# Batch 0's loads first: a gate on the summed k, w_in's second half in two DMAs, and a new order for group 0's second product

## The chip, the cores and the metric

The kernel runs on one core of a Trainium2 chip. The metric is the device time of one execution in microseconds. The kernel before has a median of 301.65 us over 5 runs (301.26 to 301.77). One further execution was profiled; it took 302.63 us, of which the profile's span is 300.8 us.

## The reference

Pooled attention over 8 batches and 8 heads feeds a two-layer network. Keys and values are averaged over blocks of 8 rows, so 576 queries meet only 72 keys:

```python
# q, k, v: (8, 8, 576, 64); w_in: (512, 2048); w_out: (2048, 512); all float32
k_p = k.reshape(B, H, 72, 8, D).mean(axis=3)
v_p = v.reshape(B, H, 72, 8, D).mean(axis=3)
attn = softmax(q @ k_p.T / 8)            # over the 72 keys
x = (attn @ v_p).transpose(0, 2, 1, 3).reshape(4608, 512)
out = gelu_tanh(x @ w_in) @ w_out        # (4608, 512) float32
```

## The kernel before, in words

**Tiling.** The attention's result is held transposed and in bf16 as `xT` (128 rows, 4 row blocks `ko`, 4608 columns). The network works on 9 groups of 512 columns, `g` = 0 to 8. In each group the *first product* (`p1_mm`, line 402) makes 16 blocks `fo` of the hidden layer, each from 4 matmuls over `ko`; ScalarE applies the gelu (`gelu`, line 408) into `gT`. The *second product* (`p2_mm`, line 411) makes 4 row tiles `r` of the output, each from 16 matmuls over `fo`; VectorE copies the sum to SBUF and SP stores it (`store`, lines 417 to 425). A matmul of 512 columns takes 0.216 us when they follow each other.

**Where attention lies.** Batch 0's attention is done alone, before the first group. Batch `g + 1` is done beside group `g`: its sums of k and v and its transposes beside the first product (the table `side`, by `fo`), its scores, exponentials, weighted sums (`av`, `av_main`) and multiplications (`mult`) between the matmuls of the second product (the table `todo`, by the place `m` in `seq`). All orders are written out by hand; every engine works through its own instructions in program order.

**Loads.** GpSimd issues q, w_in, w_out and later batches' k and v on one queue (q0 in the profile); loads that change float32 to bf16 (q, w_in, w_out) are all there. Batch 0's k and v and their remainders are issued by SP and ACT (q1 and q10). At the start GpSimd issues without any wait: q of batch 0 in two parts, w_in in two halves of two `ko` rows each (line 118), k, the remainders and q of batch 1, and w_out in four quarters of four `fo` each (line 125). There are eight semaphores for GpSimd's DMAs, and a ninth DMA waits until the one eight before it has landed; so line 125's four issues wait for both parts of q and both halves of w_in. Batch 1's v is issued by SP (line 496) after some fills on VectorE. `load_next` then loads batch 2: its q, a transposing DMA of it on SP (line 261), a small copy on GpSimd called `gate` that waits for that transpose (line 516), and behind it k and v (lines 82 to 93). Batch 2's k is summed on VectorE (line 154), transposed by a DMA on SP (line 182, into `kx`), and read by `rem_scores` (line 301) at `m` = 2 of group 1's second product.

**Batch 0's order.** k is summed (`k_steps`), transposed on TensorE and copied by VectorE (lines 217, 224, 232); the scores follow, their exponentials on ScalarE, the sums of exponentials (`den0`) and their inverses by a logarithm and an exponential (lines 359, 361). Then v is summed (`v_steps`, line 154, into `vz`), the weighted sums `av0` (line 368) and the multiplications `mult0` (line 372) fill `xT`, and group 0's first product begins. `spin` (line 431) are filler matmuls.

**Group 0.** The first 12 matmuls of its first product use `ko` 0 and 1 for `fo` 0 to 5; then come `ko` 2 and 3, block by block. Its second product goes over all four row tiles with `fo` 0 to 7 and then over all four with `fo` 8 to 15. Since only two banks of PSUM are free for it, row tiles 0 and 1 are cut: their first half is copied to SBUF (`sums`, line 639) and added when the second is stored (line 420).

Of the kernel before, what the change touches and what calls it, by code (L numbers as in the profile page):

```python
# [18 lines left out]
def kernel(  # L19
# [49 lines left out]
    def load_k(b, engs):  # L69
        rows = k[b].rearrange("h (j l) d -> (h j) (l d)", l=8)  # L70
        main = rows[0:128 * KR].rearrange("(p r) c -> p r c", r=KR)
        n = KR // len(engs)
        for i, eng in enumerate(engs):
            eng.dma_start(out=kts[b % 2][:, i * n:(i + 1) * n], in_=main[:, i * n:(i + 1) * n])
        engs[0].dma_start(out=kts[b % 2][64:128, KR], in_=rows[128 * KR:])
        rows = v[b].rearrange("h (j l) d -> j h (l d)", l=8)
        engs[-1].dma_start(out=kts[b % 2][0:64, KR], in_=rows[64:])  # L77
# [36 lines left out]
    load_q(0, 1, 2)  # L114
    make_identity(nc, identb)

    def load_w_in(i):
        nc.gpsimd.dma_start(out=w_in_b[i], in_=w_in_v[:, 2 * i:2 * i + 2])

    load_w_in(0)  # L120
    load_w_in(1)
    load_k(1, [nc.gpsimd])
    load_q(1)
    for i in range(4):
        nc.gpsimd.dma_start(out=w_out_b[:, 4 * i:4 * i + 4, :].rearrange("p j d -> p (j d)"), in_=w_out_v[:, i])
    gate = consts.tile([1, 2], BF16, name="gate")


    xT = consts.tile([128, KO, N], BF16, name="xT")
# [125 lines left out]
    def trans_q(b, i, t0, n, bank, eng):  # L255
        trans_q_mm(b, i, t0, n, bank)
        trans_q_copy(b, i, t0, n, bank, eng)
# [4 lines left out]
                                    in_=qs[b].rearrange("p i c -> p (i c)"))  # L262

    QG = [(0, 0, 5), (0, 5, 4), (1, 0, 5), (1, 5, 4)]


    es = {}
# [170 lines left out]
    def scores(c, pr, bank):  # L438
        qk(0, c, pr, bank)
        expo(0, c, pr, bank)  # L440
# [3 lines left out]
    trans_q(0, *QG[0], 5, nc.scalar)  # L444
    trans_q(0, *QG[1], 6, nc.vector)
    trans_k_copy(0, 1, 4, upper=False)
    scores(0, 0, 2)
    scores(0, 1, 0)
    spin(2, 7)
# [40 lines left out]
        nc.vector.memset(t[:, KR + 1], 0.0)  # L490
    nc.vector.memset(kTs[1][0], 0.0)
    nc.vector.memset(kTs[1][1], 0.0)

    for i in range(2):
        nc.vector.memset(vts[1][:, 2 * i, 0:1], 0.0)
    load_v(1, [nc.sync], 2)
    for w in vps:
        nc.vector.memset(w, 8.0)
    nc.gpsimd.memset(kz, 0.0)

    for fo, ko in [(fo, ko) for fo in range(6) for ko in range(2)]:
# [3 lines left out]
    for g in range(NG):  # L505
        nb = g + 1 if g + 1 < B else None
        act_set(GELU_SET)

        def load_next():

            if nb >= KX:
                nc.gpsimd.tensor_copy(out=gate, in_=eT[64:65, H - 1, 1, 0:2])  # L512
            if nb < KX:
                load_q(g + 2)
                trans_q_dma(g + 2)
                nc.gpsimd.tensor_copy(out=gate, in_=qTs[g + 2][0:1, 1, TP - 1, 0:2])
            if g + 2 >= KX:
                load_k_dma(g + 2)
            else:
                load_k(g + 2, [nc.gpsimd])  # L520
            load_v(g + 2, [nc.gpsimd])
            if nb >= KX:
                load_q(g + 2)

        if 0 < g and nb is not None and nb < KX:
            load_next()


        side = {fo: [] for fo in range(FO)}
        if nb is not None:  # L530
            kk = k_steps(nb) if nb < KX else k_steps_dma(nb)
            tk = [lambda: trans_k(nb, 4)]
            if nb > KX:
                kk.append(lambda: trans_q_dma(nb))
            kk.append(lambda: v_moves(nb))
            vv = v_steps(nb)
            if nb >= KX:
                plan = {0: kk, 7: vv[:1], 8: vv[1:]}
            elif g:
                plan = {2: kk[:1], 3: kk[1:], 7: vv[:1], 8: vv[1:], 9: tk}  # L540
            else:
                tq = [lambda a=a, i=i: trans_q(nb, *a, (5, 6, 7, 5)[i], nc.vector) for i, a in enumerate(QG)]
                plan = {0: kk[:-1], 11: kk[-1:], 12: tk, 13: tq[:1], 14: tq[1:2], 15: tq[2:3]}
            for fo, what in plan.items():
                side[fo] += what

        if g + 1 == NG:

            gLs = [kts[i // 2].rearrange("p r c -> p (r c)").bitcast(BF16)[:, i % 2 * 512:i % 2 * 512 + 512]
                   .rearrange("p (f c) -> p f c", f=4) for i in range(4)]  # L550
            for i, o in enumerate(gLs):
                side[4 * i + 3].append(lambda i=i, o=o: nc.vector.tensor_copy(  # L552
                    out=o.rearrange("p f (x t) -> p f t x", t=4),
                    in_=gTs[g][:, 4 * i:4 * i + 4, 384:].rearrange("p f (t x) -> p f t x", t=4)))

        if g == 0:
            first = [(fo, ko) for fo in range(6) for ko in (2, 3)]
        else:  # L560
            late = 3
            rest = [fo for fo in range(4) if fo != late]
            kos = (0, 2, 1) if g == 1 else (0, 1, 2)
            first = [(fo, ko) for ko in kos for fo in rest]
            first += [(fo, ko) for fo in (late, 4) for ko in kos]
            first += [(fo, 3) for fo in rest + [late, 4]]
        for fo, ko in first:
            p1_mm(g, fo, ko)
        for fo in range(FO):
            if fo >= (5 if g else 6):  # L570
                for ko in range(KO):
                    p1_mm(g, fo, ko)
            gelu(g, fo)
            for s in side[fo]:
                s()

        if g == 0:
            load_next()


        todo, sums = {}, {}

        def at(m, f, *a):
            todo.setdefault(m, []).append((f, a))

        if nb is not None:
            act_set(EXP_SET)
        if nb is not None and nb >= KX:
            at(2, rem_scores, nb)
            at(2, rem_expo, nb)  # L590

            pairs = [(0, 0), (0, 1), (1, 0), (1, 1), (0, 2), (1, 2), (0, 3), (1, 3)]
            for pr, m in enumerate((6, 17, 31, 45)):
                at(m, main_scores, nb, pr)
            for n, m in enumerate((13, 22, 28, 34, 40, 51, 56, 62)):
                at(m, av_main, nb, *pairs[n], 4 + 2 * (n % 2))
            scalar = [(6, 0, 0), (6, 1, 0), (13, 0), (18, 0, 1), (18, 1, 1), (22, 1), (28, 2), (33, 0, 2), (33, 1, 2),
                      (34, 3), (40, 4), (46, 0, 3), (51, 5), (51, 1, 3), (56, 6), (62, 7)]
            for m, *x in scalar:
                if len(x) == 2:  # L600
                    at(m, main_expo, nb, *x)
                else:
                    at(m, norm, nb, *pairs[x[0]], 4 + 2 * (x[0] % 2))
            for n, m in enumerate((24, 30, 36, 44, 49, 57, 64, 65)):
                at(m, mult, nb, *pairs[n], 4 + 2 * (n % 2))
            if g + 2 < B:
                at(3, load_next)
        elif nb is not None:
            if g == 0:
                at(2, trans_q, nb, *QG[3], 5, nc.vector)  # L610
                at(3, v_half, 1, 0)
                at(18, v_half, 1, 1)
            pos = (6, 14, 20, 27, 34, 41, 48, 55, 61)
            for i in range(len(ORDER) + 1):
                if i < len(ORDER):
                    at(pos[i], qk, nb, *ORDER[i], 2)
                if i:
                    a = (nb, *ORDER[i - 1], 4 + 2 * ((i - 1) % 2))
                    at(pos[i], av, *a)
                if i < len(ORDER):  # L620
                    at(pos[i], expo, nb, *ORDER[i], 2)
                if i:
                    at(pos[i], norm, *a)
                    at(min(pos[i] + 9, 62 if i < len(ORDER) else 65), mult, *a)

        seq = [(r, fo) for r in range(4 if g + 1 < NG else 3) for fo in range(FO)]
        if g == 0:


            seq = [(r, 4 * (2 * i + f4) + f) for i in range(2) for rs in ((0, 1), (2, 3))[::1 - 2 * i]  # L630
                   for f4 in range(2) for r in rs for f in range(4)]
        for m, (r, fo) in enumerate(seq):
            for f, a in todo.pop(m, []):
                f(*a)
            part = g == 0 and r < 2
            p2_mm(g, r, fo, o_bank(g, r), last=7 if part and fo < 8 else FO - 1, first=8 if part and fo >= 8 else 0)
            if part and fo == 7:
                sums[r] = opool.tile([128, DM], F32, name="osb")
                nc.vector.tensor_copy(out=sums[r], in_=PS[:, o_bank(g, r)])  # L639
            if fo == FO - 1:  # L640
                store(g, r, o_bank(g, r), sums.get(r) if part else None)
        for m in sorted(todo):
            for f, a in todo[m]:
                f(*a)
# [40 lines left out]
```

The softmax here doesn't subtract the row's maximum and nothing guards it: scores larger than these inputs give would overflow.

## Time and profile before

| what | value |
|---|---|
| median of 5 runs | 301.65 us |
| profiled execution, own time | 302.63 us |
| its span | 300.8 us |
| TensorE busy | 291.1 us, 97% |
| ScalarE busy | 217.2 us, 72% |
| VectorE busy | 152.6 us, 51% |
| GpSimd busy | 37.4 us, 12% |
| granted TensorE clock | 1.00 |
| DMA moved | 43.11 MB, mean 143 GB/s |
| batch 0's v landed (VectorE's wait ends) | 16.43 us |
| first matmul of the first product | 21.35 us |
| w_in's halves landed (GpSimd's waits end) | 17.69 and 23.24 us |
| first matmul of group 0's second product | 36.23 us |
| first matmul of group 1's first product | 55.04 us |

Times are from the start of the span. In rows of the timeline and of the chain the first number is the start, the second the length; `x8` counts instructions, and a bracket tells how long the engine was idle before and what ended it. A wait for several semaphores is put down to the one that came last by the profile; where that engine had long been done, it was another, often a DMA. Beside the page, the trace holds every DMA packet with its queue and every step of a DMA's semaphore; a DMA has landed when its semaphore is full.

### The profile page before, as it was taken

The page shows a single profiled execution, that of the slowest core. Times are in us where ns is not written, and L with a number is a line of the kernel's source. Part 1 is how long each engine was busy: PE and PEld are TensorE (multiplying, and loading weights), DVE is VectorE, ACT ScalarE, POOL GpSimd, SP SyncE. Part 2 cuts the span into 40 slices and gives each one's busy share as a digit, 9 for nine tenths or more (in the row PEclk, how much of TensorE's full clock was granted, in tenths as well). Part 3 has the DMA queues.
Part 4 walks back from the last instruction along what each step waited for, and adds up shares of the span by engine and source line. Part 5 has one row for each costly group of instructions (what it writes and reads, how often), then busy time and mean ns, then how long its engine had stood idle before and what let it go on. Part 6 is the DMA issues. An engine that isn't in the chain of part 4 may idle for free.

```text
span 300.8 us, 4352 instructions
## 1 busy us (share of the span) xinstructions
PE 291.1 (97%) x1496; PEld 150.9 (50%) x1525; DVE 152.6 (51%) x308; ACT 217.2 (72%) x408; POOL 37.4 (12%) x67
## 2 busy tenths in 40 slices
PE   8789999999999999999999999999999999999995
PEld 3555545554555455545554555455545555445443
DVE  3767576584576257815690659155924630111112
ACT  1587678879888898789878988798879887206500
POOL 7104002300600060005000410032000000000000
PEclk9999999999999999999999999999999999999999
DMA  7999985980798269835994399729961210121022
GB/s 223 266 243 277 247 173 104 249 205 20 175 264 170 48 163 254 174 70 122 245 204 88 92 248 215 105 50 254 235 119 34 70 44 0 36 71 36 0 64 78
DMA packets 38791, 43.11 MB, mean 143 GB/s; under 512 B 25521, under 2 KB 26161, under 8 KB 38641
## 3 DMA queue, kind: packets, MB, share of 16 engines
q0 software_dynamic: 8000, 24.39, 35.2%
q1 hardware_dynamic: 30064, 17.06, 25.1%
q10 hardware_dynamic: 704, 1.38, 1.3%
q8 instruction: 12, 0.20, 0.3%
q14 instruction: 11, 0.08, 0.1%
HBM read 36.70 MB, written 9.44 MB: 153 GB/s over the span
## 4 chain that ended last, share of the span: by engine, by line
PE 90%; DMA 5%; DVE 2%; issue 1%; ACTq 1%
PE PS L402 41%; PE PS L411 39%; DMA vt<-in_v_dram 5%; PE PS L327 4%; PE PS L316 2%; PE PS L647 1%; DVE vt L154 1%; PE PS L301 1%; PE PS L368 1%; PE PS L292 1%; ACTq L77 0%; PE PS L272 0%; PE PS L241 0%; DVE xT L345 0%; DVE osb L639 0%
## 5 line engine op out<-in xcount | busy, mean ns | idle before, releaser
L411 PE MATMUL PS<-w_out_b,gT 128*128 128x512 bf16 x543 | 134.7, 379 | 0.9 <-issue 0.2
L402 PE MATMUL PS<-xT,w_in_b 128*128 128x512 bf16 x565 | 125.7, 379 | 0.6
L408 ACT ACTIVATE gT<-PS 128x512 bf16<-128x512 f32 x144 | 79.6, 607 | 44.6 <-PE PS L402 44.6
L402 PEld LDWEIGHTS <-w_in_b 128*128 128x128 bf16 x576 | 65.0, 113 | 58.6
L411 PEld LDWEIGHTS <-gT 128*128 128x128 bf16 x560 | 53.9, 97 | 51.1 <-issue 1.7
L345 DVE TENSOR_TENSOR xT<-PS,rc 64x288 bf16<-64x288 f32 x112 | 51.0, 455 | 21.2 <-ACT rc L337 18.6
L417 DVE COPY osb<-PS 128x512 f32<-128x512 f32 x33 | 22.8, 692 | 48.4 <-PE PS L411 42.2
L322 ACT ACTIVATE eT<-PS 64x576 bf16<-64x576 f32 x48 | 30.7, 640 | 0.6
L309 DVE COPY eT<-er 8x576 bf16<-8x576 bf16 x24 | 7.3, 302 | 39.7 <-ACT er L307 39.1
L334 ACT ACTIVATE ld<-PS 64x288 f32<-64x288 f32 x56 | 22.6, 403 | 5.7 <-PE PS L327 5.2
L337 ACT ACTIVATE rc<-ld 128x288 f32<-128x288 f32 x56 | 24.8, 443 | 1.8
L379 ACT ACT_TABLE_LOAD x17 | 21.8, 1283 | 3.6 <-issue 3.3
L154 DVE TENSOR_TENSOR kt<-kt 128x1280 f32<-128x1280 f32 (+5 forms) x18 | 18.9, 1048 | 9.4 <-DMA kt<-in_v_dram 5.3
L335 ACT ACTIVATE ld<-PS 64x288 f32<-64x288 f32 x56 | 22.5, 402 | 1.4
L327 PE MATMUL PS<-eT,vp 72*128 72x288 bf16 x96 | 19.7, 285 | 0.1
L154 DVE TENSOR_TENSOR vt<-vt 128x512 f32<-128x512 f32 (+2 forms) x18 | 15.6, 864 | 2.2 <-DMA vt<-in_v_dram 1.8
L512 POOL COPY gate<-eT 1x2 bf16<-1x2 bf16 x5 | 0.9, 174 | 125.7 <-DMA eT<-er 125.7
L327 PEld LDWEIGHTS <-vp 72*128 72x128 bf16 x96 | 9.5, 98 | 11.3
L279 ACT ACTIVATE e<-PS 72x576 bf16<-72x576 f32 x16 | 9.9, 644 | 3.3 <-PE PS L272 2.9
L431 PE MATMUL PS<-idle 128*128 128x512 bf16 x30 | 9.2, 450 | 1.2 <-DVE idle L143 1.2
L316 PE MATMUL PS<-qT,kx 128*128 128x288 bf16 x48 | 9.8, 286 | 0.0
L552 DVE COPY kt<-gT 128x512 bf16<-128x512 bf16 x4 | 3.0, 743 | 11.6 <-ACT gT L408 11.6
(66 smaller groups left out, 130.9 us busy)
## 6 DMA issues: line engine op xcount, KB each, us to landing
out_dram<-osb SPq DMA_DIRECT2D x141, 64.0 KB
kt<-in_k_dram POOLq DMA_DIRECT2D x12, 512.0 KB, 7.0
vt<-in_v_dram POOLq DMA_DIRECT2D x12, 512.0 KB, 10.6
qb<-in_q_dram POOLq DMA_DIRECT2D x7, 576.0 KB, 15.0
w_in_b<-in_moe_w_in_dram POOLq DMA_DIRECT2D x2, 1024.0 KB, 16.8
w_out_b<-in_moe_w_out_dram POOLq DMA_DIRECT2D x4, 512.0 KB, 23.8
kt<-in_k_dram POOLq DMA_DIRECT2D x1, 1024.0 KB, 22.0
vt<-in_v_dram SPq DMA_DIRECT2D x4, 256.0 KB
```

The costliest lines, as they stand in the source:

```text
L154: nc.vector.tensor_tensor(out=o, in0=a, in1=b, op=ALU.add)
L322: nc.scalar.activation(out=eT[0:64, 2 * pr:2 * pr + 2, c, :], in_=PS[64 * c:64 * c + 64, 2:4, :CH], func=ACT.Exp, scale=1.0 / 64.0)
L327: nc.tensor.matmul(out=PS[:, bank + x, :CH], lhsT=window(vps[b % 2], 2 * pr + x), rhs=eT[:, 2 * pr + x, c, :], start=True, stop=True)
L334: nc.scalar.activation(out=ld[0:64], in_=PS[64:128, bank, :CH], func=ACT.Ln)
L335: nc.scalar.activation(out=ld[64:128], in_=PS[0:64, bank + 1, :CH], func=ACT.Ln)
L337: nc.scalar.activation(out=rc, in_=ld, func=ACT.Exp, scale=-1.0)
L345: nc.vector.tensor_tensor(out=xT[rows, pr, col:col + CH], in0=PS[rows, bank + x, :CH], in1=rc[rows], op=ALU.mult)
L379: nc.scalar.preload_act_table_set(name)
L402: nc.tensor.matmul(out=PS[:, h_bank(g, fo), :], lhsT=w, rhs=xT[:, ko, r0:r0 + GROUP], start=(ko == 0), stop=(ko == KO - 1))
L408: nc.scalar.activation(out=gTs[g][:, fo, :], in_=PS[:, h_bank(g, fo), :], func=ACT.Gelu_apprx_tanh)
L411: nc.tensor.matmul(out=PS[:, bank], lhsT=gTs[g][:, fo, r * 128:(r + 1) * 128], rhs=w_out_b[:, fo], start=(fo == first), stop=(fo == last))
L417: nc.vector.tensor_copy(out=osb, in_=PS[:, bank])
```

## The change

- **A gate before the loads.** The loads of w_in, of batch 1's k and q and of w_out move into `load_rest`, called after batch 0's k has been transposed and copied. In front of it GpSimd copies two elements of batch 0's summed k (`kps[0]`) into `gate`, so everything behind waits for that sum.
- **w_in in three DMAs**: rows 0 and 1 together, row 2, row 3.
- **Group 0's first product** goes over `ko` 2 for the six blocks and then over `ko` 3, not block by block.
- **Transposes of batch 1** move by one block (`tk` to block 13, the q groups to 14, 15 and `m` = 3), with the banks 6, 7, 5, 4; `v_half(1, 0)` moves from `m` = 3 to 4 and the third of the positions `pos` from 20 to 21.
- **The fill of `vps[0]`** moves ahead of batch 1's v load.
- **Group 0's second product** begins with `fo` 0 to 3 for all four row tiles, goes on with row tiles 0 and 1 through `fo` 4 to 15, four at a time, and ends with row tiles 2 and 3. Now these two are the ones cut, after `fo` 3, in banks 6 and 7.

```diff
-    def load_w_in(i):
-        nc.gpsimd.dma_start(out=w_in_b[i], in_=w_in_v[:, 2 * i:2 * i + 2])
-
-    load_w_in(0)
-    load_w_in(1)
-    load_k(1, [nc.gpsimd])
-    load_q(1)
-    for i in range(4):
-        nc.gpsimd.dma_start(out=w_out_b[:, 4 * i:4 * i + 4, :].rearrange("p j d -> p (j d)"), in_=w_out_v[:, i])
+    def load_w_in(k0, k1):
+        nc.gpsimd.dma_start(out=w_in_b[k0 // 2][:, k0 % 2:k0 % 2 + k1 - k0], in_=w_in_v[:, k0:k1])
+
     gate = consts.tile([1, 2], BF16, name="gate")
+
+    def load_rest():
+        load_w_in(0, 2)
+        load_w_in(2, 3)
+        load_w_in(3, 4)
+        load_k(1, [nc.gpsimd])
+        load_q(1)
+        for i in range(4):
+            nc.gpsimd.dma_start(out=w_out_b[:, 4 * i:4 * i + 4, :].rearrange("p j d -> p (j d)"), in_=w_out_v[:, i])
...
     QG = [(0, 0, 5), (0, 5, 4), (1, 0, 5), (1, 5, 4)]
+    QB = (6, 7, 5, 4)
...
     trans_k_copy(0, 1, 4, upper=False)
+
+    nc.gpsimd.tensor_copy(out=gate[0:1], in_=kps[0][0:1, 0, 0:2])
+    load_rest()
     scores(0, 0, 2)
...
     nc.vector.memset(kTs[1][1], 0.0)
+    nc.vector.memset(vps[0], 8.0)
...
     load_v(1, [nc.sync], 2)
-    for w in vps:
-        nc.vector.memset(w, 8.0)
+    nc.vector.memset(vps[1], 8.0)
...
-                tq = [lambda a=a, i=i: trans_q(nb, *a, (5, 6, 7, 5)[i], nc.vector) for i, a in enumerate(QG)]
-                plan = {0: kk[:-1], 11: kk[-1:], 12: tk, 13: tq[:1], 14: tq[1:2], 15: tq[2:3]}
+                tq = [lambda a=a, i=i: trans_q(nb, *a, QB[i], nc.vector) for i, a in enumerate(QG)]
+                plan = {0: kk[:-1], 11: kk[-1:], 13: tk, 14: tq[:1], 15: tq[1:3]}
...
-            first = [(fo, ko) for fo in range(6) for ko in (2, 3)]
+            first = [(fo, ko) for ko in (2, 3) for fo in range(6)]
...
-                at(2, trans_q, nb, *QG[3], 5, nc.vector)
-                at(3, v_half, 1, 0)
+                at(3, trans_q, nb, *QG[3], QB[3], nc.vector)
+                at(4, v_half, 1, 0)
                 at(18, v_half, 1, 1)
-            pos = (6, 14, 20, 27, 34, 41, 48, 55, 61)
+            pos = (6, 14, 21, 27, 34, 41, 48, 55, 61)
...
-            seq = [(r, 4 * (2 * i + f4) + f) for i in range(2) for rs in ((0, 1), (2, 3))[::1 - 2 * i]
-                   for f4 in range(2) for r in rs for f in range(4)]
+            seq = [(r, f) for r in range(4) for f in range(4)]
+            seq += [(r, 4 * f4 + f) for f4 in range(1, 4) for r in range(2) for f in range(4)]
+            seq += [(r, f) for r in (2, 3) for f in range(4, FO)]
...
-            part = g == 0 and r < 2
-            p2_mm(g, r, fo, o_bank(g, r), last=7 if part and fo < 8 else FO - 1, first=8 if part and fo >= 8 else 0)
-            if part and fo == 7:
+            part = g == 0 and r >= 2
+            if part and fo < 4:
+                p2_mm(g, r, fo, 4 + r, last=3)
+            else:
+                p2_mm(g, r, fo, o_bank(g, r), first=4 if part else 0)
+            if part and fo == 3:
                 sums[r] = opool.tile([128, DM], F32, name="osb")
-                nc.vector.tensor_copy(out=sums[r], in_=PS[:, o_bank(g, r)])
+                nc.vector.tensor_copy(out=sums[r], in_=PS[:, 4 + r])
```

## The prediction

> **What bounds the kernel now.** I read the page first. TensorE is busy 97% of the span, and the chain that ended last says the same, with one exception:
>
> ```profile
> PE 90%; DMA 5%; DVE 2%; issue 1%; ACTq 1%
> ```
>
> The 5% of DMA is one stretch. The chain of waits in order of time, cut to the first 24 us (start, length, what), shows it:
>
> ```profile
> 2.62 13.80 DMA vt<-in_v_dram
> ...
> 16.43 1.24 DVE vt L154
> ...
> 18.89 1.15 PE PS L368 x8
> 20.05 0.49 PE PS L354 x4
> 20.54 0.98 PE PS L368 x8
> 21.52 1.94 PE PS L402 x9
> ```
>
> Batch 0's v lands at 16.41 us; VectorE sums it, TensorE does its weighted sums, and the first product follows without a gap. From 21.35 to the end TensorE has hardly an idle microsecond, so only two things move the end: when the first product starts, and any new hole behind it.
>
> Why v takes 13.8 us is read from the DMA view cut to 10.1 to 12 us (queue: packets, MB, share of 16 engines). q1 and q10 are SP's and ACT's queues, with v; q0 is GpSimd's, with q and then w_in:
>
> ```profile
> q0 software_dynamic: 78, 0.22, 59.2%
> q1 hardware_dynamic: 78, 0.16, 24.3%
> q10 hardware_dynamic: 77, 0.16, 21.3%
> ```
>
> The shares add to 105%: the engines are full, each queue gets the same number of packets, and w_in's are the longer ones. Between 12 and 16.4 us v moves only its last 0.21 MB.
>
> The timeline gives what else could set the start, and the next place where a load is nearly late:
>
> ```profile
> 14.78 0.17 DVE L232 COPY kT<-PS 64x64 bf16<-64x64 bf16 x1
> 17.30 0.60 PE L431 MATMUL PS<-idle 128*128 128x512 bf16 x2
> 20.63 0.65 ACT L359 ACTIVATE ld<-PS 128x576 f32<-128x576 f32 x1 [0.76 <-PE PS L354]
> 45.87 2.81 SPq L261 DMA_TRANSPOSE qT<-qb  x1
> 50.66 0.17 POOL L516 COPY gate<-qT 1x2 bf16<-1x2 bf16 x1 [22.94 <-DMA qT<-qb]
> 51.26 1.28 POOL L82 DMA_DIRECT2D kt<-in_k_dram  x2 [0.43 <-DVE osb L417]
> 61.00 2.35 DVE L154 TENSOR_TENSOR kt<-kt 128x1280 f32<-128x1280 f32 x2 [3.71 <-DMA kt<-in_v_dram]
> 64.88 2.59 SPq L182 DMA_TRANSPOSE kx<-kz  x1
> 69.38 0.32 PE L301 MATMUL PS<-qT,kx 128*16 128x288 bf16 x4
> ```
>
> The last six rows are one chain tied to the DMA backlog, not to TensorE: batch 2's q lands (45.73), is transposed, releases the gate, batch 2's k is loaded (landed 60.98), summed, transposed (the transpose's semaphore is full at 68.87). TensorE reads kx when its previous product lets it, at 69.28. The slack is 69.28 - 68.87 - 0.05 for the signal = **0.36 us**.
>
> **The front.** The gate makes GpSimd wait for the sum of k, which ends at 8.60 (8.18 + 0.42), instead of issuing w_in at 3.03. Gate copy to first issue took 0.60 us at 50.66 to 51.26, so w_in is issued at about 9.25. From issue to first packet the rows give 1.4 us (51.26 to 52.64, engines idle) and 3.4 us (q at 1.25, first packet 4.62, engines busy with k and v): first packet at 10.6 to 12.6. But w_in lies behind q in its queue now, and its first packet is at 10.13 already. So six microseconds of later issue buy v only 0.5 to 2.5 us without w_in. The second row has the same neighbours as the new place; I take 11.6, between the two.
>
> What that is worth: at 10.1 v and the rest of its queues have 0.53 MB left (0.32 until 12, 0.21 after). Alone, the two queues moved 0.65 MB in 1.6 us (3 to 4.6 us), so 0.53 MB are 1.3 us of work. With the first packet at 10.6 about 0.2 MB go out early; 0.33 MB are left at 10.6 instead of at 11.3, and v lands near 15.7. With 11.6 or 12.6 it lands between 12 and 14.
>
> VectorE is in order: its copies end at 14.95, so the sums of v start there at best, not at 16.43. TensorE's first weighted sum comes 2.46 us after them (18.89 - 16.43): 17.41. It also has its fillers, the second of which starts at 17.52 and takes 0.22: 17.74. The gain is 18.89 - 17.74 = 1.15 us, or 0.7 with v at 15.7. Twenty matmuls at 0.123 us lead to the first product at 20.2. The others are in time: the logarithm at 20.63 then starts at 19.87, when ScalarE is free (0.76 of idle gone); the last normalised rows are ready at 21.98, needed at 20.2 + 12 x 0.216 = 22.8.
>
> The Trainium skill (DMA: Bandwidth & Descriptors, Latency and other measured facts) gives a GpSimd-issued DMA about 1 us to its first byte. By that w_in would start at 10.25, as now, and the front gain would be nothing; the rows, 1.4 and 3.4 us, are longer, and I follow them.
>
> **What waits behind GpSimd's gate.** Three loads of w_in, three for batch 1's k and v rest, one of q, four of w_out. A third w_in issue costs GpSimd 0.6 to 0.7 us, which nobody waits for: all later loads stand in a full queue. What counts is whether the engines stop. v's 1.3 us of work cover a delay of w_in from 10.13 to 11.4; beyond that the whole queue slips. With 11.6 the slip is 0.2; the bounds are 0 and 1.2. Against it:
> - w_in's last row, needed after 18 matmuls (20.2 + 3.9 = 24.1): the second half lands by 23.2 now. Covered up to 0.9 of slip; then TensorE waits for the rest.
> - Batch 1's k lands at 27.4, summed by 30.37; ScalarE's small move of it is issued after the 12th gelu (31.98 now, about 30.9 then). Covered to 0.5.
> - w_out's quarters land at 33.8, 37.0, 40.3 and 42.6 (issue time plus time to landing). Four row tiles on the first quarter need them at about 35.1, 39.5, 41.7 and 43.9: over 1.2 us of slack each. In the old order an earlier start would have had about the same for the second quarter.
>
> **Moves at no net cost.** The order of k rows in group 0's first product leaves the first gelu where it is: it needs 19 matmuls instead of 14 from a start 1.15 earlier, 24.3 us both times; seven gelus then run at ScalarE's rate (3.62 us) and the banks they free are wanted later. The transposes of batch 1's k and q are the same 23, one step later. The fill of vps ahead of batch 1's v load (0.91 us, plus 0.16) is paid by VectorE being a microsecond ahead; SP issues at 23.8 to 24.1 as now (24.9 if the front gains nothing), and that load lands near 40.85, when the sums on VectorE reach it.
>
> **The second product of group 0.** Two partial copies and two adding stores stay two and two. In the old trace TensorE loses about 0.6 us here: 0.17 at 40.29, waiting for the small move of v (landed 40.16, 8.2 after issue), and about 0.45 near 44.2 to 44.7 for the multiply that frees banks 4 and 5. Both come again about a microsecond earlier, and one is added: the plain store of row tile 0, now after its 36th matmul, puts a 0.69 us copy ahead of a multiply, and a weighted sum reads that bank five steps on. By my schedule it waits 0.25. Bounds for all of it: 0.3 gained, 0.5 lost. Arrival at group 1 without further waits: 1.15 - 0.25 = 0.9 us earlier (0.45 with v at 15.7).
>
> **Where the gain goes.** The chain of batch 2 doesn't move with TensorE. Its first link is the last load of the backlog, and the later start of w_in can only keep it or delay it. Stores compete with batch 2's k from 52.6 to 61: SP issued them at 50.5, 52.4, 54.8 and 59.5, and would at about 48.7, 50.5, 52.4 and 55.5. Two fall before k and two beside it, as now; I take 0, with 0.5 to gain and 0.3 to lose. So kx is ready at 68.92 + 0.2 = 69.1, while TensorE would be there at 68.4. It waits 0.7, and 69.28 - 69.1 = 0.2 us of the 0.9 are left. Behind it every load is released by TensorE's own progress (the gates at 75.9, 107.1 and on), so the rest is shifted as it is.
>
> Against the profiled execution: span 300.8 - 0.2 = 300.6, its own time 302.63 - 0.2 = 302.43. That execution lies 1.0 above the median of 301.65; with the median, **301.45 us**.
>
> **The rivals.**
> 1. *The chain of batch 2 comes earlier too.* If the stores moved ahead of its k leave the queues emptier, kx may be ready 0.5 earlier and 0.7 to 0.9 us get through: 300.8. For it: before 54 us the engines aren't full. Against: the bytes beside k are about the same.
> 2. *The restart leaves the engines empty.* If the first packet needs 3.4 us and all 16 engines ramp up after that, the queue slips 1.2: kx at 70.1, TensorE 0.85 late, 302.5. It decides from a slip above 0.36, and is over 0.2% above 0.96. The 3.4 us row speaks for it; against it, that the long latency may itself be the backlog, in which case nothing is empty. The Trainium skill (SBUF — State Buffer, SBUF: two separate sides) warns of this from another side: VectorE in a two-port mode keeps GpSimd from writing descriptors. No row has bf16 copies beside such an issue, as there will be from 9.11 on.
>
>    At 51.26 a multiply ran beside the issue, and the first packet still took 1.4 us.
> 3. *The gate does nothing for v*: w_in's packets start near 10.1 as before, half a microsecond ahead of the shorter row. Then the front is unchanged, kx keeps its slack, and only the reordering shows, -0.3 to 0.25: 301.35 to 301.9.
>
> **How the numbers follow.** 0.2% of 301.65 is 0.60 us, about what a measurement of this kernel can tell from no change. The forecast (gain capped by kx, -0.1 to 0.55) has 0.40, rival 3 0.10: together "same", 0.50. Rival 1 has 0.28, all faster. Rival 2 has 0.22, slower. The forecast's own range is 301.1 to 301.75. For 8 in 10 the range reaches into both sides: 300.5 to 302.4.
>
> **What would show it.** After: the wait on vt before VectorE's L154 gone or short, L368 first at about 17.7, L402 at about 20.2; the first q0 packet of w_in near 11.6; w_out's first quarter landed before 35; a new TensorE wait at L301 near 69 us, on the transpose of kx. It is wrong if L301 starts at 68.4 without waiting (rival 1), if q0 is empty for over a microsecond near 12 us (rival 2), or if TensorE waits for w_in or w_out.

## The result, and the profile after

Over 54 executions the changed kernel has a median of 302.48 us, the kernel before 301.76 us over 94. The ratio is 1.0023 (95% interval 1.0016 to 1.0029): slower by about 0.7 us, where 301.45 had been forecast and the range ended at 302.4. The profiled execution of the changed kernel took 302.43 us by its own time (span 300.5).

The front went as predicted. The timeline of the changed kernel, first GpSimd, then VectorE, then TensorE (start, length, engine, line, what; in brackets the idle time before and what ended it; the change moves the lines of the kernel down, so L154 before is L157 here):

```profile
8.58 0.17 POOL L452 COPY gate<-kp 1x2 bf16<-1x2 bf16 x1 [5.50 <-DVE kp L157]
8.70 1.80 POOL L118 DMA_DIRECT2D w_in_b<-in_moe_w_in_dram  x3
14.89 1.95 DVE L157 TENSOR_TENSOR vt<-vt 128x1024 f32<-128x1024 f32 x2
17.65 1.14 PE L372 MATMUL PS<-e,vz 72*128 72x288 bf16 x8
20.10 1.24 PE L406 MATMUL PS<-xT,w_in_b 128*128 128x512 bf16 x5
```

No wait on v stands before VectorE's sums any more; the first weighted sum (L372, predicted 17.74) starts at 17.65 and the first product (L406, predicted 20.2) at 20.10, 1.25 us earlier than in the profile before. The DMA view from 10.1 to 12 us shows why:

```profile
q10 hardware_dynamic: 148, 0.28, 43.9%
q0 software_dynamic: 55, 0.14, 39.7%
q1 hardware_dynamic: 112, 0.20, 28.2%
```

v's two queues moved 0.48 MB there instead of 0.32, and q0's share fell from 59 to 40%. By the packets, w_in's first is at 11.16 (11.6 predicted, 10.13 before), and v landed at 13.64.

The gain is gone 35 us later. VectorE, then TensorE, in group 0's second product:

```profile
41.33 1.15 DVE L157 TENSOR_TENSOR vt<-vt 128x512 f32<-128x512 f32 x2 [0.68 <-DMA vt<-in_v_dram]
43.15 1.92 DVE L349 TENSOR_TENSOR xT<-PS,rc 64x288 bf16<-64x288 f32 x4
46.90 0.69 DVE L421 COPY osb<-PS 128x512 f32<-128x512 f32 x1 [1.84 <-PE PS L415]
47.62 0.94 DVE L349 TENSOR_TENSOR xT<-PS,rc 64x288 bf16<-64x288 f32 x2
...
39.09 0.41 PE L296 MATMUL PS<-e,vp 72*128 72x288 bf16 x2 [0.22 <-DMA vp<-kp]
43.65 0.28 PE L296 MATMUL PS<-e,vp 72*128 72x288 bf16 x1 [0.61 <-DVE xT L349]
44.14 0.28 PE L296 MATMUL PS<-e,vp 72*128 72x288 bf16 x1 [0.21 <-DVE xT L349]
48.62 0.28 PE L296 MATMUL PS<-e,vp 72*128 72x288 bf16 x1 [0.21 <-DVE xT L349]
```

Two new things happen. VectorE waits 0.68 us for batch 1's v, so the multiplies that free TensorE's banks come late: the hole of TensorE near 44 us is 0.61 + 0.21 where it was 0.21 (last row below, from the profile before). And VectorE stands idle for 1.84 us behind a store copy (L421) that waits for TensorE's last matmul of row tile 0, while the multiply queued behind it (L349 at 47.62) has had its factors since 45.34 (end of ScalarE's `rc`); TensorE waits for that multiply at 48.62.

```profile
44.71 0.28 PE L292 MATMUL PS<-e,vp 72*128 72x288 bf16 x1 [0.21 <-DVE xT L345]
```

The second product takes 19.97 us (34.97 to 54.94) instead of 18.81. Group 1 starts at 54.94, before at 55.04: of 1.25 us earlier, 0.10 are left.

The third predicted place, TensorE at `kx`, shows no wait:

```profile
69.28 0.44 PE L305 MATMUL PS<-qT,kx 128*16 128x288 bf16 x8
```

`kx` had landed at 68.46. In the profile before, the same matmuls start at 69.38, so here too 0.10 us are left.

Of the 0.3 us between the two profiled spans (300.8 and 300.5) this explains 0.1; most of the rest lies between 179 and 211 us, in group 5, where nothing was changed (31.26 us there before, 31.08 after). And profiled executions don't explain the medians: the one of before lies 0.9 above its median, the one of after at its median. The experiments are about that.

### The profile page after: what moved, and what is told of

Its sections match the earlier page's. It is cut to its first block, busy times and chain, and to the rows that moved or that the text cites. A ratio compares the mean times of both kernels' runs of the same rounds, so it can differ in the third digit from the quotient of the medians.

```text
span 300.5 us, 4352 instructions
## 1 busy us (share of the span) xinstructions
PE 290.9 (97%) x1496; PEld 150.9 (50%) x1525; DVE 152.7 (51%) x308; ACT 216.7 (72%) x408; POOL 38.0 (13%) x69
## 4 chain that ended last, share of the span: by engine, by line
PE 84%; DMA 7%; DVE 3%; ACT 3%; issue 1%; SPq 1%; DVEq 0%
PE PS L415 38%; PE PS L406 37%; DMA vt<-in_v_dram 5%; PE PS L331 4%; PE PS L320 2%; DMA kt<-in_k_dram 2%; PE PS L658 1%; ACT e L283 1%; PE PS L276 1%; PE PS L305 1%; ACT rc L365 1%; DVE kt L157 1%; ACT ld L363 1%; DVE xT L349 1%; SPq L93 1%
## 5 line engine op out<-in xcount | busy, mean ns | idle before, releaser
L406 PE MATMUL PS<-xT,w_in_b 128*128 128x512 bf16 x565 | 125.6, 379 | 0.6
L406 PEld LDWEIGHTS <-w_in_b 128*128 128x128 bf16 x576 | 65.1, 113 | 58.7
L349 DVE TENSOR_TENSOR xT<-PS,rc 64x288 bf16<-64x288 f32 x112 | 51.0, 455 | 19.7 <-ACT rc L341 17.1
L421 DVE COPY osb<-PS 128x512 f32<-128x512 f32 x33 | 22.8, 692 | 50.0 <-PE PS L415 46.7
L338 ACT ACTIVATE ld<-PS 64x288 f32<-64x288 f32 x56 | 22.6, 403 | 5.8 <-PE PS L331 5.2
L157 DVE TENSOR_TENSOR kt<-kt 128x1280 f32<-128x1280 f32 (+5 forms) x18 | 18.9, 1048 | 9.9 <-DMA kt<-in_v_dram 5.8
L157 DVE TENSOR_TENSOR vt<-vt 128x512 f32<-128x512 f32 (+2 forms) x18 | 15.6, 865 | 1.4 <-DMA vt<-in_v_dram 1.1
L559 DVE COPY kt<-gT 128x512 bf16<-128x512 bf16 x4 | 3.0, 744 | 11.6 <-ACT gT L412 11.6
## 6 DMA issues: line engine op xcount, KB each, us to landing
vt<-in_v_dram POOLq DMA_DIRECT2D x12, 512.0 KB, 10.1
```

The source lines that it names most:

```text
L157: nc.vector.tensor_tensor(out=o, in0=a, in1=b, op=ALU.add)
L338: nc.scalar.activation(out=ld[0:64], in_=PS[64:128, bank, :CH], func=ACT.Ln)
L349: nc.vector.tensor_tensor(out=xT[rows, pr, col:col + CH], in0=PS[rows, bank + x, :CH], in1=rc[rows], op=ALU.mult)
L406: nc.tensor.matmul(out=PS[:, h_bank(g, fo), :], lhsT=w, rhs=xT[:, ko, r0:r0 + GROUP], start=(ko == 0), stop=(ko == KO - 1))
L421: nc.vector.tensor_copy(out=osb, in_=PS[:, bank])
```

## Experiments

Two theories stood at the start. **A**: every execution of before loses about 1.1 us at the front, the gate wins it, and the new second product costs more than that. **B**: only the profiled execution of before was so late; others start nearly as early as the changed kernel, so there was little to win, and the rest of the change costs its 0.7 us openly. All runs below are ratios to the kernel before on the same chip.

**1. Kernel before, once more.** No edit.

> The kernel before, unchanged, for a second profiled execution of it. Theory A (the new second product of group 0 gives the front's gain back): this execution looks like the first one, first product near 21.3 us, group 0's second product near 18.8 us long (36.23 to 55.04 there), ratio 1.000 +- 0.001. Theory B (the profiled execution of before was untypically late at the front, so there was less to gain): the first product starts near 20.5, v's wait on VectorE is shorter than 1.48 us, span near 299.9 instead of 300.8; ratio the same.

Median 301.73, ratio 1.0001 (0.9988 to 1.0014). Its profile is as long as the first (span 300.8, own time 302.67) and quite different. The chain of waits in order of time (start, length, what):

```profile
11.74 26.81 DMA w_out_b<-in_moe_w_out_dram
...
65.48 4.04 DMA kx<-kz
```

And TensorE's rows of its timeline:

```profile
23.29 8.82 PE L402 MATMUL PS<-xT,w_in_b 128*128 128x512 bf16 x40 [0.46 <-DMA w_in_b<-in_moe_w_in_dram]
38.59 1.45 PE L411 MATMUL PS<-w_out_b,gT 128*128 128x512 bf16 x6 [0.64 <-DMA w_out_b<-in_moe_w_out_dram]
69.57 0.44 PE L301 MATMUL PS<-qT,kx 128*16 128x288 bf16 x8 [0.28 <-DMA kx<-kz]
```

Here v landed at 15.13, VectorE waited 0.36 for it, and the first product started at 20.07, without any gate. This execution lost its time to w_in, w_out and `kx` instead. One profile had shown one draw of where the DMA backlog is late.

**2. The gate alone.** Before, with `load_rest` behind the gate, w_in in three DMAs and `ko` 2 ahead of `ko` 3; second product, transposes and fills as before.

```diff
...
+    nc.gpsimd.tensor_copy(out=gate[0:1], in_=kps[0][0:1, 0, 0:2])
+    load_rest()
...
-            first = [(fo, ko) for fo in range(6) for ko in (2, 3)]
+            first = [(fo, ko) for ko in (2, 3) for fo in range(6)]
```

> The kernel before with the loads of the change alone: the gate, w_in in three DMAs, and ko 2 before ko 3 in the first product; old second product, old banks, old fills. A: first product near 20.1, group 0's second product 18.6 to 19.0 long, group 1 at about 53.9, time 0.7 to 1.1 us below before. B: first product near 20.1 as well, but only 0 to 0.4 us below before. If neither, w_out's second quarter, needed at the ninth matmul, stops TensorE and shows as a wait on w_out near 37 us.

Median 301.92, ratio 1.0010 (0.9995 to 1.0024): no gain. First product at 20.08, but then TensorE's timeline has

```profile
38.31 1.46 PE L414 MATMUL PS<-w_out_b,gT 128*128 128x512 bf16 x6 [1.00 <-DMA w_out_b<-in_moe_w_out_dram]
...
69.41 0.44 PE L304 MATMUL PS<-qT,kx 128*16 128x288 bf16 x8 [0.41 <-DMA kx<-kz]
```

The old order wanted w_out's second quarter at 37.31 here, and it landed at 38.27. The prediction gave that order "about the same" slack as the new one; behind the gate it has none. In the nine profiles of kernels with the gate the quarter landed at 36.45 to 38.47 (mean 37.49), in the eleven without it at 35.66 to 38.55 (mean 36.63; these kernels differ in other places too), and in experiments 5 and 9, with the old order and an early TensorE but no gate, nothing waited for it. So kernels with the gate get w_out later, by 0.9 us on the mean, as well as TensorE earlier. The new order has a purpose, and the gate without it gained nothing here; this one profile also waited for `kx`.

**3. The change without its gate.** The loads go out at the start, in the same order; all else as changed.

```diff
+    load_rest()
...
-    nc.gpsimd.tensor_copy(out=gate[0:1], in_=kps[0][0:1, 0, 0:2])
-    load_rest()
```

> The changed kernel with its loads issued at the start, without the gate: all of the rest of the change stays. A: first product near 21.3 as before, second product of group 0 near 20 us long as in the changed kernel, so 0.9 to 1.3 us above before (302.7 to 303.1). B: first product near 20.5, 0.6 to 0.9 above before.

Median 302.59, ratio 1.0034 (1.0020 to 1.0048). In its profile v landed at 15.12 and the first product started at 20.28, again without a gate. The slow part of the change is what is left here; against this the gate gives back 0.0011, about 0.3 us, where this ratio alone has an interval of 0.0014 to either side.

**4. The fill put back.** Changed kernel, `vps[0]`'s fill behind batch 1's v load again.

```diff
-    nc.vector.memset(vps[0], 8.0)
...
     load_v(1, [nc.sync], 2)
-    nc.vector.memset(vps[1], 8.0)
+    for w in vps:
+        nc.vector.memset(w, 8.0)
```

> The changed kernel with the fill of vps[0] back behind batch 1's v load. SP issues that load near 22.8 instead of 23.78. A: its last part lands 0.6 to 0.9 earlier than 41.24, VectorE's wait before it (0.68) goes, TensorE's wait at the weighted sum near 43.65 (0.61) shrinks, and 0.3 to 0.7 us below the changed kernel comes out (301.8 to 302.2). B: says the same of the place, and nothing of the size. If the landing is set by the full DMA queues and not by the issue, nothing moves.

Median 302.14, ratio 1.0018 (1.0005 to 1.0031). SP issues the load at 22.84 instead of 23.77, it lands at 40.38 instead of 41.24, and VectorE's rows have no wait before the sums and still the idle 1.84 us at the store copy:

```profile
41.03 1.15 DVE L157 TENSOR_TENSOR vt<-vt 128x512 f32<-128x512 f32 x2
46.60 0.69 DVE L421 COPY osb<-PS 128x512 f32<-128x512 f32 x1 [1.84 <-PE PS L415]
```

The second product is 19.53 us long: 0.44 less than in the changed kernel. The median is 0.34 lower; the ratios differ by 0.0005, within their intervals.

**5. Nothing of v at the front.** Before, with batch 0's `v_steps` reading k's rows, so that no wait on v is possible (the weighted sums of batch 0 are of k instead of v; v is loaded all the same).

```diff
-        t = vts[b % 2]
+        t = vts[b % 2] if b else kts[0][:, 0:4]
```

> The kernel before, with batch 0's sums of v reading batch 0's k rows instead of v (batch 0's v is still loaded, but not used): no wait on v is possible. Theory A (every execution of before loses about 1.1 us at its first product waiting for v): the first product starts near 20.1 and the time falls by 0.4 (held by batch 2's transposed k) to 1.1 us, to 300.7-301.4. Theory B (only the profiled execution was that late, the others start at about 20.1 anyway): same time as before, ratio within 0.9992 to 1.0005.

Median 301.53, ratio 0.9989 (0.9974 to 1.0005). First product at 20.00 in the profile, which then waited 0.36 for `kx`. By the middle of the interval 0.3 us are to be had at the front, not 1.1; none of its 12 executions was over 302.1, of the 35 of before beside it eight were over 302.3. The time still holds whatever `kx` takes back; experiment 18 is about that.

**6. The new second product alone.** Before, with the new `seq`, its cut row tiles, the banks `QB`, `pos` and `plan`; loads, fills and first product as before.

```diff
...
+            seq = [(r, f) for r in range(4) for f in range(4)]
+            seq += [(r, 4 * f4 + f) for f4 in range(1, 4) for r in range(2) for f in range(4)]
+            seq += [(r, f) for r in (2, 3) for f in range(4, FO)]
...
+            part = g == 0 and r >= 2
```

> The kernel before with only the new order of group 0's second product, its banks and the moved transposes of batch 1; loads, fills and the first product's order as before. Theory B: this is about half of the change's cost, +0.3 to +0.5 us (302.1-302.3), the rest being the fill ahead of batch 1's v load. Theory A (the front gain is real and the new second product costs 1.5 or more on top of it): +1.1 to +1.5, 302.9-303.3. If the order costs nothing and the fill is all: 301.8.

Median 302.19, ratio 1.0021 (1.0001 to 1.0041). That is 0.63 us by the ratio and 0.49 by the medians (301.70 beside it). The second product takes 19.33 us in its profile, and VectorE's row that matters is there again:

```profile
47.03 0.69 DVE L418 COPY osb<-PS 128x512 f32<-128x512 f32 x1 [1.84 <-PE PS L412]
47.76 0.94 DVE L346 TENSOR_TENSOR xT<-PS,rc 64x288 bf16<-64x288 f32 x2
```

**7. The multiply ahead of the store copy.** Changed kernel.

```diff
-                    at(min(pos[i] + 9, 62 if i < len(ORDER) else 65), mult, *a)
+                    at(35 if (g, i) == (0, 3) else min(pos[i] + 9, 62 if i < len(ORDER) else 65), mult, *a)
```

> The changed kernel with one edit: in group 0 the multiply that stands behind row tile 0's store copy on VectorE (place 36) is put ahead of it (place 35). If that copy is what holds TensorE near 48.6 us: that wait of 0.2 to 0.45 goes, group 0's second product takes about 19.5 instead of 19.97 us, and the time is 302.1 (ratio to before about 1.001). If the copy hides behind TensorE's own order (rival: the hole moves to the next multiply): 302.4-302.5, as the changed kernel.

Median 302.12, ratio 1.0018 (0.9998 to 1.0038). VectorE's multiply now starts at 45.25 behind `rc`, the copy follows in its idle time, and TensorE's wait near 48.6 is gone; the hole near 44 (0.68 + 0.21) stays, since the fill is still ahead. Second product 19.62 us. The median is 0.36 below the changed kernel's; the ratios differ by 0.0005, within their intervals.

```profile
45.25 0.94 DVE L349 TENSOR_TENSOR xT<-PS,rc 64x288 bf16<-64x288 f32 x2 [0.31 <-ACT rc L341]
46.78 0.69 DVE L421 COPY osb<-PS 128x512 f32<-128x512 f32 x1 [0.59 <-PE PS L415]
```

**8. Both.** Edits 4 and 7 together.

> The changed kernel with both edits: vps[0]'s fill back behind batch 1's v load, and the multiply ahead of row tile 0's store copy. Theory B (nothing was to be gained at the front in typical executions; fill 0.35 and multiply 0.4 are the whole cost): 301.7-301.8, as before, ratio 0.999 to 1.0005; second product near 19.1. Theory A: below before, 300.9-301.4, since the front gain of 1.1 is kept and its cost removed. If the multiply doesn't matter: 302.1, as with the fill alone.

Median 301.78, ratio 0.9993 (0.9970 to 1.0016): as before. Second product 18.97 us. The two edits take away 0.7 us, all that the change had cost. Theory A needed 301.4 or less. But TensorE's rows held something else, so the time alone doesn't rule A out:

```profile
68.89 0.44 PE L305 MATMUL PS<-qT,kx 128*16 128x288 bf16 x8 [0.56 <-DMA kx<-kz]
```

The predicted cap appears as soon as TensorE is early enough. From this reading to the end of the span it is 231.2 us in this kernel, in the changed one and in experiment 5, 231.4 in the first profile of before: whatever delays this matmul delays the end.

**9. The fill alone.** Before, with `vps[0]`'s fill ahead of the load.

```diff
+    nc.vector.memset(vps[0], 8.0)
     for i in range(2):
         nc.vector.memset(vts[1][:, 2 * i, 0:1], 0.0)
     load_v(1, [nc.sync], 2)
-    for w in vps:
-        nc.vector.memset(w, 8.0)
+    nc.vector.memset(vps[1], 8.0)
```

> The kernel before with only the fill of vps[0] moved ahead of batch 1's v load. Theory B (the cost of the change is a sum: the new second product 0.5 and this fill 0.35): batch 1's v is issued and lands about 0.9 us later, VectorE's second half of its sums starts late, and the time is 302.0-302.1. Rival (the later v costs only together with the new second product, whose multiplies have less room): 301.7-301.8.

Median 302.32 against 301.63 beside it, ratio 1.0012 (0.9994 to 1.0031). The two differ: 0.69 us by the medians, 0.36 by the ratio, whose interval reaches below 1. SP issues at 23.82 instead of 22.64 (experiment 1), and the wait on VectorE and the hole on TensorE are those of the changed kernel:

```profile
41.31 1.15 DVE L154 TENSOR_TENSOR vt<-vt 128x512 f32<-128x512 f32 x2 [0.69 <-DMA vt<-in_v_dram]
...
43.63 0.28 PE L292 MATMUL PS<-e,vp 72*128 72x288 bf16 x1 [0.63 <-DVE xT L345]
```

**10 and 11. Batch 1's v earlier still**, ahead of the fills of `kps` and `kTs`, in the kernel before and in that of experiment 8.

> The kernel before with batch 1's v load issued ahead of the fills of kps and kTs, about 0.7 us earlier. If the second half of that v's sums holds the multiply that frees banks 4 and 5 (the 0.45 us hole in group 0's second product): that hole shrinks by up to 0.3 and the time is 301.4-301.6. If the hole is set by the logarithms on ScalarE instead: 301.7, as before.

> The changed kernel with the fill back, the multiply ahead of row tile 0's store copy, and batch 1's v load also ahead of the fills of kps and kTs (0.7 us earlier). If the load of v still sets VectorE's second half of sums: the remaining hole near 43.5 us shrinks by up to 0.3, second product 18.7 instead of 18.97, time 301.4-301.6. If not: 301.75, as without the move. Theory A would have both below 301.2.

The first: 301.75, ratio 1.0000 (0.9983 to 1.0017), second product 18.96. The second: 302.70, ratio 1.0035 (1.0015 to 1.0056), which neither theory had. In its profile the second product is no shorter in the part that was meant (its 0.21 hole stays), and TensorE waits 0.93 for `kx`: batch 2's q was transposed at 46.30 and `kx` read at 69.32, against 46.00 and 68.89 in experiment 8. Whether the earlier load made the later one late isn't shown: in other profiles with the gate that transpose starts at 45.39 to 46.37. Of the 0.9 us in the medians the profile shows 0.4; the rest stays open.

**12 to 15. The cap by `kx` lifted, first try.** The first reading of `kx` three matmuls (0.65 us) later, the first weighted sum and its norm at 16 instead of 13, in four kernels.

```diff
...
+            rl = 3 if nb == 2 else 0
-            at(2, rem_scores, nb)
-            at(2, rem_expo, nb)
+            at(2 + rl, rem_scores, nb)
+            at(2 + rl, rem_expo, nb)
...
-            for n, m in enumerate((13, 22, 28, 34, 40, 51, 56, 62)):
+            for n, m in enumerate((13 + rl, 22, 28, 34, 40, 51, 56, 62)):
...
-                at(3, load_next)
+                at(3 + rl, load_next)
```

> The kernel before, with batch 2's kx read three matmuls later (0.65 us): its remainder scores at m = 5 of group 1's second product, the first weighted sum and its norm at 16, the next loads behind them. If kx caps most executions (waits of 0.28 to 0.56 seen in profiles): 301.2-301.4, ratio 0.998 to 0.999. If TensorE's own arrival sets the time in most executions: 301.65, as before.

> The changed kernel with the same edit. Its TensorE reached kx at 69.28, 0.8 after kx had landed, so both theories say no change: 302.4-302.6. A fall below 302.2 would mean that kx also limits typical executions of the changed kernel.

> The changed kernel with the fill back, the multiply ahead of the store copy and kx read three matmuls later. In its profile TensorE waited 0.56 for kx. If kx is its cap: 301.2-301.3, ratio to before 0.998. If the front gain of the gate was real and only held back by kx, it is also below before_kx3 by up to 0.4. If neither: 301.75.

> The kernel before without use of batch 0's v (its sums read k's rows) and with kx read three matmuls later. If the front wait exists in typical executions and only kx hid it: 300.8-301.1, at least 0.3 below before_kx3. If the front wait exists only in a few executions: the same as before_kx3 within 0.15, with fewer long executions.

All four came out slower than the same kernels without the edit; to before, the ratios are 1.0020 (1.0011 to 1.0029), 1.0044 (1.0032 to 1.0056), 1.0013 (0.9998 to 1.0028) and 1.0008 (0.9995 to 1.0022). The edit had a price of its own, seen in the fourth kernel's row as in the others':

```profile
74.14 0.41 PE L327 MATMUL PS<-eT,vp 72*128 72x288 bf16 x2 [0.27 <-ACT eT L322]
```

The later norm holds up ScalarE's next exponential; from group 1's second product to group 2's first one it is 17.69 us instead of 17.27, so 0.4 us of the 0.6 that each of the four lost by its ratio (0.0019 to 0.0021). In the third kernel TensorE still waited 0.16 for `kx`. The try priced nothing else.

**16 to 18. The same by two matmuls**, weighted sums left in place: `rl = 2`, used for `rem_scores`, `rem_expo` and `load_next` only.

> The kernel before, with the remainder scores of batch 2 (first reading of kx) at m = 4 instead of 2 of group 1's second product, and the next loads behind them; the weighted sums stay. If kx caps typical executions: 301.3-301.4 (up to 0.43 less). If it does so only in a few: 301.6-301.8. If the edit has a cost of its own as the longer move had: group 1's second product is over 17.3 us long in the profile, and the difference is taken off.

> The repaired changed kernel (fill back, multiply first) with kx read two matmuls later; its profile waited 0.56 for kx. If kx caps its typical executions: 301.35-301.45. If not: 301.75.

> The kernel before without use of batch 0's v, with kx read two matmuls later. If typical executions of before lose over 0.3 at the front and kx hides it: 301.0-301.2. If they start as early as this anyway: equal to before_kx2 within 0.2.

Here group 1's second product is 17.27 us long in the first and third, as without the edit: no price of its own. Before: 301.97, ratio 1.0002 (0.9990 to 1.0013); the cap by `kx` does not set typical executions of before. Without v: 301.43, ratio 0.9992 (0.9981 to 1.0002), and no wait for `kx` in its profile. That is 0.25 us at the front against before, and 0.5 by the medians against experiment 16, which has the same edit; neither expectation had that, and the interval reaches zero. So theory A is out in its size: with `kx` not in the way the front is worth 0.3 to 0.5 us, not 1.1. Theory B holds in the main, with a front that is worth a little more than nothing.

The repaired kernel: 301.66, ratio 0.9991 (0.9982 to 1.0000), between its two expectations. It is the best that uses v, by 0.1% and at the edge of what can be told. But in its profile the cap wasn't lifted:

```profile
69.22 0.44 PE L305 MATMUL PS<-qT,kx 128*16 128x288 bf16 x8 [0.75 <-DMA kx<-kz]
```

TensorE began group 1 at 53.63, 1.4 us before the first profile of before, and then gave 0.75 back. What the repaired kernel would take with an earlier `kx` stays open.

## Why the prediction was wrong

**The first step that failed is the front's gain as a term for all executions.** The trace showed 16.43 for the end of the wait on v, and the working took 1.15 us from it; then "That execution lies 1.0 above the median of 301.65" took 301.45 from 302.43 by subtracting a constant, as if every execution had that wait and the 1.0 lay elsewhere. The profiles taken for the experiments let the draws be counted:

| kernels | v landed | first product starts |
|---|---|---|
| 8 profiles without the gate, v used | 15.03, 15.12, 15.13, 15.86, 15.92, 16.00, 16.16, 16.41 | 20.07 to 21.35, mean 20.70 |
| 9 profiles with the gate | 12.84 to 13.78 | 19.85 to 20.51, mean 20.12 |
| 3 profiles that don't use v | not needed | 19.94 to 20.11, mean 20.02 |

With the gate VectorE starts its sums at 14.64 to 15.31. The first profile of before was the latest of eight. The gate won 0.58 us on the mean of profiled executions. In the times the front is worth only 0.2 to 0.5 us: 0.0011 between the changed kernel and experiment 3, 0.0011 and 0.0008 in experiments 5 and 18, each with an interval of 0.001 or more to either side, and medians 0.4 and 0.5 apart between experiments 12 and 15 and between 16 and 18. Part of the difference is that the profiled executions without the gate are late ones: the eight lie 0.36 us above their kernels' medians on average, the nine with the gate 0.10. Why is not shown. In the mechanism at the front nothing was off: later packets of w_in, v landed in time, TensorE's next steps at the predicted microsecond.

**The second term that failed, and the larger one in the median, is the second product with its fill.** The prediction gave it -0.25 us, with bounds of 0.3 gained and 0.5 lost, and the fill nothing. In the trace it lost 1.16 us. In the times experiment 3, which has both and no gate, measured 0.0034 (1.0 us); less the gate's 0.0011 that is the 0.0023 of the result. With the gate's 0.3 us and a cost of 0.25 the median would have been near 301.7, inside the range; the cost of 1.0 us is what took it to 302.48. How it divides is less firm. By the ratios the new second product has 0.0021 (0.63 us) and the fill 0.0012 (0.36 us), by the medians beside them 0.49 and 0.69; each single ratio has an interval of some 0.002 to either side. That the two make up the cost is shown by experiment 8, where both repairs together bring the time back to that of before. Two steps of the working were mis-sized:

- The store copy ahead of the multiply was seen, and put at a wait of 0.25 us. Experiment 7 took off 0.35 us in the profile (19.97 to 19.62) and 0.36 in the median (302.48 to 302.12). The bracket shows a wait of 0.21, but the second matmul of the pair, which without a wait starts 0.13 behind the first (0.28 and 0.41 in all), started 0.49 behind it (48.13 and 48.62): that is 0.36 lost.
- The fill was "paid by VectorE being a microsecond ahead", and SP would issue "at 23.8 to 24.1 as now". It did, at 23.77; but "now" was the execution with the longest wait on v. With the fill behind it the load is issued at 22.6 to 22.7 where that wait is short or absent (22.64, 22.61 and 22.70 in experiments 1, 5 and 8), and at 23.23 to 23.53 in the profiles of experiments 6, 12 and 16, with waits of 1.1 to 1.3. So an early front lets the load go out earlier too, and the fill takes 0.9 us of that away (22.84 in experiment 4, 23.77 here). The load landed at 41.24, 0.6 after VectorE was ready for it (40.65), not at 40.85. The same late execution served as the base twice.

**The cap by `kx`** was to hold 0.7 us back. The reading was taken to start at 69.28 in the profile before, where its row has 69.38. `kx` landed at 68.46 rather than at 69.1: against the first profile the backlog had not slipped (w_in's last row landed at 22.75, no later than its second half had before, and the first issue followed the start of the gate copy by 0.12 us and not by 0.60). TensorE, late by its own holes, came after it. Over all profiles there is a slip, and it is larger than the 0.2 us of the working: `kx` landed at 67.58 to 69.53 (mean 68.31) in the eleven without the gate and at 68.46 to 69.37 (mean 68.93) in the nine with it, 0.6 us later, in kernels that differ in other places too. So the load that caps TensorE does move, and where TensorE is early it waits: 0.41, 0.56, 0.93, 0.16 and 0.75 us in experiments 2, 8, 11, 14 and 17. The cap was right in kind, and experiment 16 shows that it isn't what limits typical executions of before.

**The rivals.** Rival 2 named 302.5, which is the time measured, by a mechanism that did not occur: q0 was never empty near 12 us, and nothing waited for w_in. Rival 3 was wrong as well, v did come earlier. In this profile `kx` did come 0.41 earlier than in the first one, as rival 1 had it, but TensorE wasn't there to use it. That the profiled execution's own time was forecast as 302.43 and measured as 302.43 is luck: the forecast's 0.2 us was to be 1.15 less 0.25 less the cap's 0.7; what came was 1.25 less 1.16, and the other 0.1 from places that the change doesn't touch.

**The rule weighed in the prediction.** The Trainium skill (DMA: Bandwidth & Descriptors, Latency and other measured facts) gives a GpSimd-issued DMA about 1 us to its first byte. Here the first packet of w_in came 2.46 us after the issue (8.70 to 11.16), with the 16 engines full; the measurement decides, and the row of 1.4 us on idle engines and that of 3.4 us on busy ones did bracket it. As to VectorE's copies beside such an issue, the profile of before does have rows, which the prediction missed: w_out's issues at 8.74 and 11.79 stand beside bf16 copies (L224 at 9.11 and 12.00) and take 0.56 and 0.54 us, against 0.53 at 17.69 and 23.24 without such copies. After, the three issues of w_in beside such copies take 1.80 us, 0.60 each. No issue was stretched; whether the first packet came later for it, no run here shows.

## What to carry to other kernels

When the profiled execution lies above the median by more than the gain that is claimed, the wait it shows may be the reason that it lies there: profile the same kernel again before a wait on a DMA is counted as a gain, and subtract the gain from the profiled execution only, never from the median as well. An in-order engine that copies results out for a store can hold up work that is long ready: place the multiply that frees a bank ahead of a copy that waits for TensorE, and read the idle time before the copy, not only the wait it causes. Moving work ahead of a load's issue is paid for where the load is consumed, here over 17 us later.

## What was not expected of the hardware

Executions of one and the same kernel are late in different places. Batch 0's v landed anywhere from 15.03 to 16.41 us in the eight profiles whose loads go out at the start, at 15.13 and 16.41 in the two of before itself; w_out's second quarter kept TensorE for 0.64 us in one execution of before and not at all in another, and yet both spans were 300.8 us. The medians of before agree within 0.2 us from one set of runs to the next (301.63 to 301.80), so the spread sits inside the executions: the middle half of 154 of them lies between 301.5 and 302.1 us.
